# Batch 0's k and v as head pairs of nine tokens a partition, q and the first layer 1 by token halves, and the steps up to tile 1 in a written order by engine

## The chip, the cores and the metric

The kernel runs on one core of a Trainium2 chip. TensorE (PE) multiplies matrices into PSUM; VectorE (DVE), ScalarE (ACT) and GpSimd (POOL) work elementwise; SyncE (SP), ACT and POOL issue DMAs that share 16 DMA engines. Each engine takes its own instructions in the order in which they were written, and waits on semaphores of the others. The metric is the device time in microseconds (us) of the whole program.

## The reference

Inputs are q, k, v of shape (8 batches, 8 heads, 576 tokens, 64), four experts' w1 (512 x 1024) and w2 (1024 x 512), and 4608 x 4 probabilities.

```python
def phi(x):
    return np.where(x > 0, x, np.exp(x) - 1.0) + 1.0
q_p, k_p = phi(q), phi(k)
kv = np.einsum('bhsd,bhse->bhde', k_p, v)
z = np.sum(k_p, axis=2)
num = np.einsum('bhsd,bhde->bhse', q_p, kv)
den = np.einsum('bhsd,bhd->bhs', q_p, z)[..., None] + 1e-06
x = (num / den).transpose(0, 2, 1, 3).reshape(B * S, H * D)

p = domain_probs / (domain_probs.sum(-1, keepdims=True) + 1e-09)
for e in range(4):
    h = np.maximum(x @ w1[e], 0.0)
    out += p[:, e:e + 1] * (h @ w2[e])
```

So a linear attention per batch makes x (4608 tokens x 512), and four two-layer networks are run on every token and summed with the token's probabilities.

## The kernel before

The 4608 tokens are nine tiles of 512. Tile j below 8 is the first 512 tokens of batch j; the ninth collects the 64 leftover tokens of every batch. All products are in half precision.

**Attention of a batch.** q, k and v come in pieces of two heads (256 KB), four tokens a partition, and the leftovers in pieces of their own (`load`, `load_left`). phi is min(exp(x), max(x + 1, 1)): ACT makes the exp (`phi_act`), DVE the rest (`phi_dve`). `kv` multiplies k and v of a head pair into a 64 x 65 block for each head (column 65 is the sum z); ACT copies it to `kvz`. `pe_qT` transposes q on TensorE. `nd` makes numerators and denominators of a head pair and token block, `norm` divides on DVE (a reciprocal, L474, and a product, L475). `pe_xT` transposes the quotient to `xT`, which the networks read. From batch 2 on the transposes are DMAs.

**The networks.** Layer 1 of expert 0 on tile 0 is plain (`layer1_group`, L552), and so is layer 2 of all four experts on tile 0 (`layer2_part`, L607). All else is a seven-product scheme by 2 x 2 blocks: products p1 to p7 of layer 1 in `Block` (TensorE L761, copies and relus on ACT, add-relu on DVE, L745), layer 2 in `layer2_product` (L696), with sums of weights on DVE (`weight_sums` s, `weight_sums2` t), of tokens (`token_sum`, ts), and of hidden values on POOL (`hidden_sum`). `add_acc` adds a layer-2 product, scaled by the probability, to the output accumulator on DVE (L598) or, the first time, on ACT (L596).

**Weights and batch 1** are loaded by POOL, in the order of `CFG["DMA"]`: w1 of expert e in halves (`w1e0`, `w1e1`; expert 0's in quarters, `w100` to `w103`), w2 in halves (`w2e0`, `w2e1`), each converted to half precision on the way. A DMA that POOL issues takes one of eight semaphores, and waits until the DMA that had it eight issues before has landed; SP and ACT share another eight.

**What sets the order.** Nothing is scheduled by the compiler. Batch 0 is written out step by step from `CFG["B0"]` (loads) and `CFG["START"]`, where a number is that many filler matmuls on zeros (`warm`, L888) and `dma0` and `dma1` are POOL's load list. All other steps have a due position in `CFG` and are sorted by it: one list for all engines, so what a step issues on TensorE, and what ACT or DVE does with its product, stand at the same place of the list. PSUM tiles of the attention take turns in banks: `s`, `e`, `b`, `py` in the start, then `s` alone (two buffers).

Of the kernel before, what the change touches and what calls it, by code (L numbers as in the profile page):

```python
# [1 line left out]

# [8 lines left out]
FP32 = mybir.dt.float32  # L11
# [9 lines left out]
    "DMA": ('w100', 'w101', 'w102', 'w103', 'k0', 'w201', 'lk1', 'w200', 'w111', 'w110', 'w121', 'w120', 'lv0', 'lk0', 'w211', 'w210', 'v2', 'v1', 'v0', 'k1', 'w130', 'lv1', 'w131', 'q0', 'k2', 'k3', 'v3', 'w220', 'q2', 'q1', 'w221', 'q3', 'w230', 'w231'),  # L21
# [51 lines left out]
    "MODE": {'k0': 0, 'q2': 1, 'k3': 0, 'q0': 0, 'k2': 0, 'k1': 1, 'q1': 0, 'q3': 0, 'T3': 0, 'T0': 0, 'T1': 1, 'v1': 2, 'v2': 0, 'v3': 2, 'v0': 0, 'T2': 1},  # L73
    "APS": ('s', 'e', 'b', 'py'),
    "START": (11, 'qa1', 'qa0', 'ka0', 'qd1', 'lv', 'qd0', 2, 'qT1', 'kd0', 5, 'qT0', 'ka1', 'v1', 'lka', 'lkd', 'v0', 7, 'kv0', 'qa2', 'kd1', 'ka2', 'qa3', 3, 'nd0', 'kd2', 7, 'kv1', 'qd2', 'v2', 'qd3', 'dma0', 'v3', 4, 'nd1', 'qT2', 1, 'kv2', 'ka3', 3, 'xT0', 'dma1', 'kd3', 'qT3', 'nd2', 'xT1', 1, 'kv3', 'ph1', 1, 'nd3', 'ph2', 'xT2', 'xT3', 1, 'ph0'),
    "B0": ('slk', 'aq0', 'slv', 'aq1', 'sv0', 'sv1', 'sq2', 'sk2', 'ak0', 'sq3', 'sv2', 'sv3', 'ak1', 'sk3'),
    "CAST": (),
}
# [3 lines left out]
def kernel(  # L82
# [10 lines left out]
    nc = tc.nc  # L93
    CAST = CFG["CAST"]
    ATTN, HSUM, L2ORD, L2AT, MODE = (CFG[x] for x in ("ATTN", "HSUM", "L2ORD", "L2AT", "MODE"))
# [32 lines left out]
    make_identity(nc, identh)  # L128

# [14 lines left out]
    w1_sb = [pw.tile([P, DC, F], FP16, tag=f"w1_{e}", name=f"w1_{e}") for e in range(E)]  # L144
    w2_sb = [pw.tile([P, FC, Dm], FP16, tag=f"w2_{e}", name=f"w2_{e}") for e in range(E)]
# [5 lines left out]
    s1_sb = [pw.tile([P, 3, 2, F // 2], FP16, tag=f"s1_{e}", name=f"s1_{e}") for e in range(E)]  # L151


    t2_sb = {e: pw.tile([P, 3, FH, DH], FP16, tag=f"t2_{e}", name=f"t2_{e}") for e in SE}
# [9 lines left out]
    turn = {"aps": ["s", "e"], "ph": ["b", "py"]}  # L164

    def bank(kind, shape, dtype, name):
        tag = turn[kind][0]
        turn[kind] = turn[kind][1:] + [tag]
        return ppm.tile(shape, dtype, tag=tag, bufs=2, name=name)

    def aps(shape, dtype, name):
        return bank("aps", shape, dtype, name)
# [888 lines left out]
```

## Time and profile before

| | us |
|---|---|
| median of 3 runs (495.6 to 497.83) | 495.95 |
| span of the profiled execution | 494.1 |
| TensorE busy | 483.7 |
| DVE busy | 379.5 |
| POOL busy | 357.0 |
| ACT busy | 336.7 |

The page gives no time of the profiled execution beside its span; the median of the runs lies 1.85 us above it. A span is the time from the first to the last instruction on the core. A row of a timeline has start, length, engine, line, operation and tiles, and in brackets how long the engine stood idle before it and what ended that. A busy engine isn't always a useful one: fillers count, and matmuls are pipelined, so that a row's length is longer than its share of the engine. The granted clock in the profile is 1.00 in every stretch; what TensorE really did at the start is seen in the distance of its rows.

The transfers behind the start, by size and median time from issue to landing:

| issued | queue | count | KB each | us to landing |
|---|---|---|---|---|
| q, k, v pieces of later batches | SP | 26 each | 256 | 2.8 to 3.2 |
| weights in halves | POOL | 14 | 512 | 12.2 |
| w1 of expert 0 in quarters | POOL | 4 | 256 | 5.7 |

### The profile page before, as it was taken

To read this page: it belongs to the slowest core of one execution; us is meant where nothing else is said; L and a number is where in the kernel's file an instruction comes from. 1 tells how busy PE (TensorE), PEld (TensorE's weight loads), DVE (VectorE), ACT (ScalarE), POOL (GpSimd) and SP (SyncE) were. 2 spreads that over 40 slices of the span, in tenths; PEclk is the share of its full clock that TensorE was granted. 3 is DMA by queue.
4 is the path that set the end of the run, shared out by engine and by line. 5 is a ranking of instruction groups with operands and counts; after the bars stand their busy time and mean duration, and the time that the engine had idled before them with its cause. 6 is when DMAs were issued, how large, how long until landed. Compare 5 with 4: busy or idle time off the path is not lost.

```text
span 494.1 us, 11611 instructions
## 1 busy us (share of the span) xinstructions
PE 483.7 (98%) x4346; PEld 409.3 (83%) x4346; DVE 379.5 (77%) x800; ACT 336.7 (68%) x678; POOL 357.0 (72%) x344
## 2 busy tenths in 40 slices
PE   9999999999999999999999999999999999999996
PEld 3557656878898989898989898989898888888885
DVE  5639988799867987698859886888687756775686
ACT  6768969954988488848894789468954565446530
POOL 3735204878977797769776977698669877987775
PEclk9999999999999999999999999999999999999999
DMA  8999966542465234533464255523231020002003
GB/s 261 222 214 247 262 134 189 161 106 49 110 188 116 55 111 161 132 69 93 134 165 82 71 150 139 102 53 94 87 74 35 4 96 1 1 1 87 1 1 86
DMA packets 82104, 53.65 MB, mean 109 GB/s; under 512 B 46240, under 2 KB 75808, under 8 KB 82048
## 3 DMA queue, kind: packets, MB, share of 16 engines
q1 hardware_dynamic: 70512, 40.00, 31.0%
q0 software_dynamic: 9888, 11.41, 12.2%
q10 hardware_dynamic: 1648, 1.51, 1.1%
q8 instruction: 34, 0.56, 0.5%
q14 instruction: 22, 0.18, 0.1%
HBM read 45.16 MB, written 9.44 MB: 111 GB/s over the span
## 4 chain that ended last, share of the span: by engine, by line
PE 79%; DMA 11%; DVE 5%; ACT 3%; POOL 1%; issue 1%; SPq 0%; ACTq 0%; DVEq 0%
PE py L696 37%; PE pb L761 21%; PE pe L761 16%; DMA w<-in_moe_w_dram 9%; DVE acc L598 2%; PE py L607 1%; DMA rawb<-in_v_dram 1%; DVE x_sb L475 1%; PE psum_nd L492 1%; PE psum_kv L444 1%; DVE h L745 1%; POOL w L185 1%; DMA rawh<-in_q_dram 1%; PE pb L696 1%; ACT u L772 0%
## 5 line engine op out<-in xcount | busy, mean ns | idle before, releaser
L598 DVE SCALAR_TENSOR_TENSOR acc<-py,p_sb,acc 128x256 f32<-128x256 f32 (+1 forms) x382 | 182.4, 488 | 44.3 <-PE py L696 39.6
L745 DVE CUSTOM_DVE_ANT_0 h<-pe,u 128x512 f16<-128x512 f32 x140 | 96.4, 688 | 44.1 <-PE pe L761 26.1
L761 PEld LDWEIGHTS <-w 128*128 128x128 f16 x1120 | 108.9, 98 | 17.3 <-issue 1.2
L663 POOL TENSOR_TENSOR hs<-h 128x512 f16<-128x512 f16 x64 | 74.2, 1159 | 54.4 <-DVE h L745 53.3
L696 PEld LDWEIGHTS <-h 128*128 128x128 f16 x1024 | 99.6, 98 | 12.3 <-issue 0.9
L696 PE MATMUL py<-w,h 128*128 128x256 f16 x744 | 106.4, 273 | 0.0
L772 ACT COPY u<-pb 128x512 f32<-128x512 f32 x140 | 83.0, 593 | 27.4 <-PE pb L761 25.5
L665 POOL TENSOR_TENSOR hs<-hs,h 128x512 f16<-128x512 f16 x64 | 74.3, 1160 | 27.5 <-PE py L696 24.9
L761 PEld LDWEIGHTS <-s 128*128 128x128 f16 x840 | 81.6, 98 | 11.9
L761 PE MATMUL pb<-tt,w 128*128 128x256 f16 x560 | 84.0, 273 | 0.1
L696 PEld LDWEIGHTS <-hs 128*128 128x128 f16 x768 | 74.4, 98 | 8.8 <-issue 0.4
L669 POOL TENSOR_TENSOR hs<-h,hs 128x512 f16<-128x512 f16 x64 | 75.3, 1177 | 3.6 <-PE py L696 3.2
L696 PE MATMUL py<-t,hs 128*128 128x256 f16 x496 | 74.4, 273 | 0.1
L667 POOL TENSOR_TENSOR h<-h 128x512 f16<-128x512 f16 x64 | 74.3, 1162 | 0.0
L787 ACT ACTIVATE h<-pe 128x512 f16<-128x512 f32 x70 | 42.0, 600 | 45.0 <-PE pe L761 44.2
L781 ACT COPY pe<-pb 128x512 f32<-128x512 f32 x70 | 40.1, 573 | 41.6 <-PE pb L761 15.4
L805 ACT ACTIVATE h<-pb 128x512 f16<-128x512 f32 x70 | 42.1, 601 | 9.6 <-PE pb L761 9.5
L761 PE MATMUL pe<-tt,s 128*128 128x256 f16 x280 | 42.0, 273 | 0.0
L761 PE MATMUL pb<-tt,s 128*128 128x256 f16 x280 | 42.0, 273 | 0.0
L761 PE MATMUL pb<-xT,w 128*128 128x256 f16 x248 | 37.2, 273 | 0.4 <-DMA w<-in_moe_w_dram 0.4
L761 PE MATMUL pe<-xT,w 128*128 128x256 f16 x248 | 37.2, 273 | 0.3 <-ACT pe L781 0.3
L761 PE MATMUL pe<-xT,s 128*128 128x256 f16 x248 | 37.2, 273 | 0.0
(125 smaller groups left out, 609.6 us busy)
## 6 DMA issues: line engine op xcount, KB each, us to landing
out_dram<-acc SPq DMA_DIRECT2D x32, 256.0 KB, 2.5
w<-in_moe_w_dram POOLq DMA_DIRECT2D x14, 512.0 KB, 12.2
rawb<-in_v_dram SPq DMA_DIRECT2D x26, 256.0 KB, 2.8
rawb<-in_q_dram SPq DMA_DIRECT2D x26, 256.0 KB, 2.8
rawb<-in_k_dram SPq DMA_DIRECT2D x26, 256.0 KB, 3.2
w<-in_moe_w_dram POOLq DMA_DIRECT2D x4, 256.0 KB, 5.7
rawb<-in_k_dram POOLq DMA_DIRECT2D x4, 256.0 KB, 8.0
rl<-in_q_dram SPq DMA_DIRECT2D x16, 64.0 KB, 2.7
```

The costliest lines, as they stand in the source:

```text
L598: nc.vector.scalar_tensor_tensor(out=acc, in0=ps, scalar=pscal, in1=acc, op0=AO.mult, op1=AO.add)
L663: nc.gpsimd.tensor_tensor(out=hs[0], in0=a21, in1=a22, op=AO.add)
L665: nc.gpsimd.tensor_tensor(out=hs[1], in0=hs[0], in1=a11, op=AO.subtract)
L667: nc.gpsimd.tensor_tensor(out=a21, in0=a11, in1=a21, op=AO.subtract)
L669: nc.gpsimd.tensor_tensor(out=hs[3], in0=a12, in1=hs[1], op=AO.subtract)
L696: nc.tensor.matmul(out=ps, lhsT=lhsT(k), rhs=rhs[:, k], start=first and k == 0, stop=k == FH - 1, skip_group_check=True,)
L745: nc.vector._custom_dve(TENSOR_ADD_SAT, out=out, in0=ps, in1=u, s0=BIG, s1=0.0)
L761: nc.tensor.matmul(out=ps[:, kk], lhsT=lk(kc), rhs=rhs[:, kc], start=first and kk == 0 and kc == 0, stop=kc == 1, skip_group_check=True,)
L772: nc.scalar.copy(u, self.b)
L781: nc.scalar.copy(self.e5, self.b)
L787: nc.scalar.activation(self.h[:, :, 0, 0:NH], self.e5, AF.Relu)
L805: nc.scalar.activation(self.h[:, :, 1, 0:NH], self.b, AF.Relu)
```

## The change

- **Batch 0's k and v.** All 576 tokens of a head pair are one piece of 128 partitions (64 for each head) with nine tokens each, so a run of memory is 2,304 bytes and there are no leftovers of k and v to load. `kv` is nine times two matmuls of 64 x 65, one for each head, on the two halves of the partitions. The raw and converted tiles stand where the weights and weight sums of experts 2 and 3 come later. The exp is always in SBUF (`k_exp`, ACT), max(x + 1, 1) is on DVE or POOL (`k_lin`), the minimum on DVE (`k_min`), the cast of v on POOL or ACT (`v_cast`), and the copy of each head's block on ACT and DVE.
- **Batch 0's q** is loaded, mapped and transposed by token halves and four heads, in runs of 512 bytes; two of the four `q_lin` are on POOL. The transposes of x are by token halves too (`x_half`), with copies on ACT or DVE.
- **Layer 1 of expert 0 on tile 0** works by token halves (`layer1_half`): 64 matmuls of 256 columns for 32 of 512, cut where the parts of `xT` come (`CUT`).
- **Fillers**: 8, 4 and 2, for 46 before.
- **The order.** Steps are split where another engine takes over (`yield`): the TensorE part, the part on ACT or DVE, the store. `CFG["EARLY"]` names the parts one by one, from the first load to tile 1's first two experts; behind it the due positions rule as before. In it expert 1's w1 (`w110`, `w111`) is loaded right after expert 0's, ahead of both halves of expert 0's w2; before, `w201` and `w200` came first.
- **Banks.** A step's PSUM tile takes the bank named for it in `BANK`, otherwise `s`.

```diff
+    "LQ": 'SSSS',
+    "LK": 'ASSS',
+    "LV": 'SSSA',
+    "KL": 'VVPV',
+    "VC": 'PPAP',
+    "QL": 'PPVV',
+    "QT": 'AVAV',
+    "KC": ('AV', 'AV', 'AV', 'AV'),
+    "XT": ('AV', 'VV', 'AA', 'AA'),
+    "CUT": (((0, 3, 4), (0, 3, 4), (0, 4), (0, 4)), ((0, 2, 4),) * 4),
+    "WARM": (8, 4, 2),
...
+    "EARLY": (
+        "lq0 ql0 lk0 lk1 ke1 lv3 qe0 lv1 kl1 km1 warm0 lv0 qm0 warm1 lq3 vc1 w100 ke0 ql3 qT0 lq2 kv1 qT0 warm2 qe3 lk3 ke3 kv1 kl0 lq1 qe1 qm3 w102 qT3 vc0",
+        "qe2 km0 ql2 kv0 kv0 kl3 lk2 ql1 ke2 kv1 kv0 qT3 qm2 qT2 qT2 km3 lv2 w101 kl2 w103 nd10 w110 vc3 nd00 vc2 km2 nd11 w111 w200 kv2 nd00 kv2 nd10 nd11",
+        "nd01 w201 kv3 k2 kv3 xT00 w120 xT00 qm1 qT1 nd01 kv2 kv3 xT10 qT1 xT01 xT01 xT11 xT11 nd31 nd31 nd21 L21 nd30 w121 L11 nd21 L01 nd20 xT10 xT21 xT21",
+        "xT31 rv0 rv1 xT31 ts0.0 L31 L01 L11 nd30 nd20 xT20 v2 xT30 ts0.1 L31 L11 ts0.2 L01 xT20 L21 s1.0 s1.1 xT30 p1.010 s1.3 L00 L00 L31 L30 p1.011 L21 rk1",
+        "L10 L10 p1.010 p2.010 p6.010 L00 p1.011 L10 p2.011 rk0 lpr0 L20 pr0 k1 w210 p6.010 k0 k3 ts0.3 L30 v3 p2.010 p2.011 p6.011 p7.010 w211 p5.010 p7.010",
+        "s0.0 p6.011 y0.00 y0.01 p4.010 p4.010 p5.011 p7.011 c22.010 s1.2 v0 p3.010 s0.3 y0.20 y0.21 v1 L20 p3.010 p7.011 b1.k2 y0.22 p1.020 p1.020 y0.02 y0.03",
+        "y0.03 c22.011 p3.011 p4.011 p2.020 p2.020 y0.10 b1.km2 q3 y0.11 y0.12 p4.011 q0 b1.v2 w130 y0.13 y0.13 s2.0 w131 b1.lv s2.1 q2 p6.020 p1.021 p6.020",
...
-    "START": (11, 'qa1', 'qa0', 'ka0', 'qd1', 'lv', 'qd0', 2, 'qT1', 'kd0', 5, 'qT0', 'ka1', 'v1', 'lka', 'lkd', 'v0', 7, 'kv0', 'qa2', 'kd1', 'ka2', 'qa3', 3, 'nd0', 'kd2', 7, 'kv1', 'qd2', 'v2', 'qd3', 'dma0', 'v3', 4, 'nd1', 'qT2', 1, 'kv2', 'ka3', 3, 'xT0', 'dma1', 'kd3', 'qT3', 'nd2', 'xT1', 1, 'kv3', 'ph1', 1, 'nd3', 'ph2', 'xT2', 'xT3', 1, 'ph0'),
-    "B0": ('slk', 'aq0', 'slv', 'aq1', 'sv0', 'sv1', 'sq2', 'sk2', 'ak0', 'sq3', 'sv2', 'sv3', 'ak1', 'sk3'),
...
+    kraw = [pw.tile([P, 2, TK, D], FP32, tag=f"{x}_{E - 1}", name=f"kraw{x}") for x in ("s1", "t2")]
+    vraw = [pw.tile([P, 2, TK, D], FP32, tag=f"{x}_{E - 2}", name=f"vraw{x}") for x in ("s1", "t2")]
+    kpos = pw.tile([P, NPAIR, TK, D], FP16, tag=f"w1_{E - 1}", name="kpos")
+    kexp = pw.tile([P, NPAIR, TK, D], FP16, tag=f"w2_{E - 1}", name="kexp")
+    vpos = pw.tile([P, NPAIR, TK, DE], FP16, tag=f"w2_{E - 2}", name="vpos")
+    nc.gpsimd.memset(vpos[:, :, :, D:DE], 1.0 / SX)
...
-    turn = {"aps": ["s", "e"], "ph": ["b", "py"]}
-
-    def bank(kind, shape, dtype, name):
-        tag = turn[kind][0]
-        turn[kind] = turn[kind][1:] + [tag]
-        return ppm.tile(shape, dtype, tag=tag, bufs=2, name=name)
+    now = [None]
 
     def aps(shape, dtype, name):
-        return bank("aps", shape, dtype, name)
-
+        return ppm.tile(shape, dtype, tag=CFG["BANK"].get(now[0], "s"), bufs=2, name=name)
...
+    class First(Batch):
+
+        def open(self):
+            self.qp = pm.tile([P, CM, H, D], FP16, tag="h", bufs=NHB, name="qp")
+            self.qT = pa.tile([P, CM, NPAIR, P], FP16, tag="qT", bufs=1, name="qT")
+            self.x = pm.tile([P, NPAIR, CM, P], FP16, tag="tt", bufs=2, name="x_sb")
+            self.new_xT()
+
+        def load_kv(self, name, i, eng):
+            t, src = {"k": (kraw, k), "v": (vraw, v)}[name]
+            eng.dma_start(
+                out=t[i // 2][:, i % 2].rearrange("p t d -> p (t d)"),
+                in_=src[0, 2 * i : 2 * i + 2].rearrange("h (p t) d -> (h p) (t d)", t=TK),
+            )
+
+        def load_q(self, i, eng):
+            t = praw.tile([P, HG, 2, D], FP32, tag="raw", name="rawq")
+            hf, g = divmod(i, 2)
+            eng.dma_start(
+                out=t,
+                in_=q[0, g * HG : (g + 1) * HG, 0:SM].rearrange("h (p c) d -> p h c d", c=CM)[
+                    :, :, 2 * hf : 2 * hf + 2
+                ],
+            )
+            self.raw["q", i] = t
+
+        def flat(self, t, i):
+            return t[:, i].rearrange("p t d -> p (t d)")
+
+        def raw_of(self, t, i):
+            return self.flat(t[i // 2], i % 2)
+
+        def k_exp(self, i):
+            nc.scalar.activation(self.flat(kexp, i), self.raw_of(kraw, i), AF.Exp)
+
+        def k_lin(self, i, eng):
+            eng.tensor_scalar(self.flat(kpos, i), self.raw_of(kraw, i), 1.0, 1.0, AO.add, AO.max)
+
+        def k_min(self, i):
+            kp = self.flat(kpos, i)
+            nc.vector.tensor_tensor(out=kp, in0=self.flat(kexp, i), in1=kp, op=AO.min)
+
+        def v_cast(self, i, eng):
+            (eng.copy if eng is nc.scalar else eng.tensor_copy)(vpos[:, i, :, 0:D], vraw[i // 2][:, i % 2])
+
+        def q_part(self, i):
+            hf, g = divmod(i, 2)
+            return self.qp[:, 2 * hf : 2 * hf + 2, g * HG : (g + 1) * HG].rearrange("p c h d -> p h c d")
+
+        def q_exp(self, i):
+            ee = self.ph["q", i] = pm.tile([P, HG, 2, D], FP16, tag="hs0", bufs=2, name="ee")
+            nc.scalar.activation(ee, self.raw["q", i], AF.Exp)
+
+        def q_lin(self, i, eng):
+            eng.tensor_scalar(self.q_part(i), self.raw["q", i], 1.0, 1.0, AO.add, AO.max)
+
+        def q_min(self, i):
+            nc.vector.tensor_tensor(out=self.q_part(i), in0=self.ph["q", i], in1=self.q_part(i), op=AO.min)
+
+        def q_turn(self, i, eng):
+            hf, g = divmod(i, 2)
+            ps = aps([P, 2, 2, P], FP16, "psum_qT")
+            for c in range(2):
+                for a in range(2):
+                    h0 = g * HG + 2 * a
+                    nc.tensor.transpose(out=ps[:, c, a], in_=self.qp[:, 2 * hf + c, h0 : h0 + 2], identity=identh)
+            yield
+            (eng.copy if eng is nc.scalar else eng.tensor_copy)(
+                out=self.qT[:, 2 * hf : 2 * hf + 2, 2 * g : 2 * g + 2], in_=ps
+            )
+
+        def kv(self, i, engs):
+            ps = aps([P, DE], FP32, "psum_kv")
+            for t in range(TK):
+                for u in range(2):
+                    us = slice(u * HP, (u + 1) * HP)
+                    nc.tensor.matmul(
+                        out=ps[us],
+                        lhsT=kpos[us, i, t],
+                        rhs=vpos[us, i, t],
+                        start=t == 0,
+                        stop=t == TK - 1,
+                        skip_group_check=True,
+                    )
+            for u in range(2):
+                yield
+                us = slice(u * HP, (u + 1) * HP)
+                (engs[u].copy if engs[u] is nc.scalar else engs[u].tensor_copy)(
+                    out=self.kvz[us, i, u], in_=ps[us]
+                )
+
+        def x_half(self, i, hf, eng):
+            ps = aps([P, 2, P], FP16, "psum_xh")
+            for c in range(2):
+                nc.tensor.transpose(out=ps[:, c], in_=self.x[:, i, 2 * hf + c], identity=identh)
+            yield
+            (eng.copy if eng is nc.scalar else eng.tensor_copy)(
+                out=self.xT[:, i, hf * NH : (hf + 1) * NH],
+                in_=ps.rearrange("p c i -> p (c i)"),
+            )
+
+    def layer1_half(g, hf, hT, cuts):
+        ps = aps([P, 2, NH], FP32, "ph")
+        for lo, hi in zip(cuts, cuts[1:]):
+            for kk in range(2):
+                fj = 2 * g + kk
+                for dc in range(lo, hi):
+                    nc.tensor.matmul(
+                        out=ps[:, kk],
+                        lhsT=w1_sb[0][:, dc, fj * P : (fj + 1) * P],
+                        rhs=b0.xT[:, dc, hf * NH : (hf + 1) * NH],
+                        start=kk == 0 and dc == 0,
+                        stop=dc == DC - 1,
+                        skip_group_check=True,
+                    )
+            yield
+        nc.scalar.activation(hT[g % 2][:, :, g // 2, hf * NH : (hf + 1) * NH], ps, AF.Relu)
...
+        @property
+        def h(self):
+            if self.hT[self.d] is None:
+                self.hT[self.d] = new_h()
+            return self.hT[self.d]
...
         def p1(self):
-            self.h = self.hT[self.d] = new_h()
             self.b = self.bank("b")
             x = xT_of(self.j)
             self.products(self.b, lambda k: a_block(self.e, 0, 0, k), x[:, 0:2, 0:NH], True)
+            yield
             self.e5 = self.bank("e")
...
-        warm_ps = ppm.tile([P, NT], FP32, tag="py", bufs=2, name="warm_ps")
+        warm_ps = ppm.tile([P, NT], FP32, tag="e", bufs=2, name="warm_ps")
...
-        for x in CFG["START"]:
-            f, *a = (warm, x) if isinstance(x, int) else steps[x]
-            f(*a)
...
+            put_at(0, f"lq{i}", b0.load_q, i, on[CFG["LQ"][i]])
+            put_at(0, f"lk{i}", b0.load_kv, "k", i, on[CFG["LK"][i]])
+            put_at(0, f"lv{i}", b0.load_kv, "v", i, on[CFG["LV"][i]])
+            put_at(0, f"ke{i}", b0.k_exp, i)
+            put_at(0, f"kl{i}", b0.k_lin, i, on[CFG["KL"][i]])
+            put_at(0, f"km{i}", b0.k_min, i)
+            put_at(0, f"vc{i}", b0.v_cast, i, on[CFG["VC"][i]])
+            put_at(0, f"qe{i}", b0.q_exp, i)
+            put_at(0, f"ql{i}", b0.q_lin, i, on[CFG["QL"][i]])
+            put_at(0, f"qm{i}", b0.q_min, i)
+            put_at(0, f"qT{i}", b0.q_turn, i, on[CFG["QT"][i]])
+            put_at(0, f"kv{i}", b0.kv, i, [on[y] for y in CFG["KC"][i]])
+            for hf in range(2):
+                put_at(0, f"nd{i}{hf}", b0.nd, i * CM + 2 * hf, 2)
+                put_at(0, f"xT{i}{hf}", b0.x_half, i, hf, on[CFG["XT"][i][hf]])
+                put_at(0, f"L{i}{hf}", layer1_half, i, hf, hT, CFG["CUT"][hf][i])
+        for x in CFG["DMA"]:
+            put_at(0, x, load_second, x)
+        for i, n in enumerate(CFG["WARM"]):
+            put_at(0, f"warm{i}", warm, n)
...
-        for _, _, g in work:
-            g[0](*g[1:])
+        live = {name: g for _, _, name, g in work}
+        assert len(live) == len(work)
+
+        def advance(name):
+
+            now[0] = name
+            g = live[name]
+            if isinstance(g, tuple):
+                g = live[name] = g[0](*g[1:]) or iter(())
+            if next(g, live) is live:
+                del live[name]
+
+        for name in " ".join(CFG["EARLY"]).split():
+            advance(name)
+        for name in [w[2] for w in work]:
+            while name in live:
+                advance(name)
 
 
 # ---- launch: one core; inputs and outputs as the reference has them ----
```

## The prediction

> **What bounds the kernel now.** I read the page first (shares of busy time), then the busy time of every engine in stretches, then the timelines of TensorE, VectorE (DVE), ScalarE (ACT) and GpSimd (POOL) up to 120 us, the chain that ended last, and the transfers.
>
> The page, then busy time by stretch; columns are the stretch, its length, and busy us with counts for PE, weight load, DVE, ACT and POOL, then clock, DMA share and GB/s:
>
> ```profile
> PE 483.7 (98%) x4346; PEld 409.3 (83%) x4346; DVE 379.5 (77%) x800; ACT 336.7 (68%) x678; POOL 357.0 (72%) x344
> ```
>
> ```profile
> 0.00:20.00 20.00, 18.55 (x119) 9.37 (x120) 13.40 (x39) 12.93 (x28) 11.47 (x26) 1.00 1.07 248
> 20.00:30.00 10.00, 10.00 (x47) 4.38 (x45) 1.36 (x6) 6.12 (x11) 3.68 (x6) 1.00 1.18 213
> 30.00:60.00 30.00, 29.25 (x224) 20.86 (x224) 26.61 (x44) 26.33 (x54) 12.23 (x17) 1.00 1.18 247
> 60.00:65.00 5.00, 4.54 (x34) 2.79 (x35) 3.50 (x6) 4.38 (x10) 0.00 (x0) 1.00 1.21 213
> 65.00:70.00 5.00, 3.83 (x32) 1.94 (x30) 4.61 (x16) 1.70 (x3) 0.00 (x0) 1.00 0.86 192
> 70.00:100.00 30.00, 29.64 (x247) 22.22 (x246) 25.15 (x43) 28.82 (x64) 17.87 (x16) 1.00 0.49 146
> 100.00:115.00 15.00, 13.89 (x136) 12.22 (x134) 14.33 (x33) 8.28 (x18) 10.62 (x10) 1.00 0.53 111
> 115.00:400.00 285.00, 284.88 (x2707) 256.21 (x2705) 228.17 (x493) 204.51 (x416) 230.35 (x209) 1.00 0.39 99
> ```
>
> TensorE is the bound from 115 us on, and nothing of the change lies there. Before that its busy share hides much, because fillers (`warm`) count as busy. So I count useful time: four 256-column matmuls take 0.44 us in the chain, 0.1094 us per 256 columns; all matmuls but the fillers, by shape and start time, make 467.0 us. The span is 494.1, so 27.1 us are lost: 15.2 up to 20 us, 1.9 from 20 to 65, 2.1 from 65 to 70, 2.5 from 70 to 115, 0.8 from there to the last matmul at 489.5, and 4.6 behind it. The change can only touch the first four, 21.7 us.
>
> TensorE's first rows, the end of batch 0's dependent work, and two stalls behind it:
>
> ```profile
> 1.19 5.58 PE L888 MATMUL warm_ps<-qz 128*128 128x512 f16 x13 [1.19 <-DVE qz L134]
> 6.83 1.24 PE L888 MATMUL warm_ps<-qz 128*128 128x512 f16 x5
> ...
> 19.96 6.21 PE L552 MATMUL ph<-xT,w 128*128 128x512 f16 x28
> 30.50 0.61 PE L761 MATMUL pb<-xT,w 128*128 128x256 f16 x4 [0.44 <-DMA w<-in_moe_w_dram]
> ```
>
> ```profile
> 30.54 0.69 DVE L633 TENSOR_TENSOR s<-w 128x1024 f16<-128x1024 f16 x1 [8.51 <-DMA w<-in_moe_w_dram]
> ```
>
> ```profile
> 60.83 1.45 PE L607 MATMUL py<-w,h 128*128 128x512 f16 x6 [0.47 <-DMA w<-in_moe_w_dram]
> ...
> 68.00 0.29 PE L492 MATMUL psum_nd<-kvz,qT 128*128 128x130 f16 x2 [0.26 <-DVE x_sb L475]
> ```
>
> The reader sees: layer 1 runs dense only from 19.96; DVE stands idle 8.51 us because expert 1's first-layer weights come after expert 0's second layer; a weight is late at 60.8; and batch 1's numerators each wait for DVE's division of the one before. From 30 to 115 us DVE is busy 74.2 us of 85 (the five rows above), so it is nearly a second bound.
>
> **The change part by part.**
>
> *Batch 0's loads.* Before: twelve 256 KB pieces in 1 KB runs and four 64 KB leftover pieces in 256-byte runs. The last k piece, issued at 8.37, lands 5.6 us later, at 13.95. From 4 to 8 us, with leftovers in flight, 283 GB/s moved; from 8 to 12, without, 348. After: eight k and v pieces of 288 KB in 2,304-byte runs, no leftovers for k and v, and four q pieces in 512-byte runs. 2.36 MB at 348 takes 6.8 us and 1.05 MB at 283 to 348 takes 3.0 to 3.7; from the first packets at about 2 us that ends at 12 to 12.5. But POOL now issues w100 and w102 behind its q step and its cast of v pair 1, at about 6.5 us instead of 10.16, so 0.5 MB written goes between: 2.7 us, by the 1.35 us a piece that four of them show (5.7 us to landing each, issued 0.8 us apart). The last v thus lands at 12 to 14.8; I take 14. SP issues the last q, k and v pieces only as lq0, lk1 and lv1 land, and ACT issues lv3 behind the exp of k pair 1; SP's issues before were paced in the same way (5.0 to 8.9 us), and the DMA engines are full meanwhile (share 1.07), so these waits cost nothing unless the queue runs dry, 0.7 us for a piece. Batch 2's loads on SP keep their number and wait for the same buffers.
>
> *What follows the last load.* POOL carries three `tensor_scalar` steps and three v casts now, with seven weight issues of 0.75 us between them. A cast of 512 costs it 0.67; a two-operand step 1.16. For a `tensor_scalar` that the trace does not show I take 0.7 (it has one input, like the cast); 1.16 is the other end, 1.4 us more over three. The cast of v pair 3 stands behind w103 and w110: about 16 us. Then 18 matmuls of kv (0.5 to 1 us), two copies (0.27 and about 0.2), numerators and division (0.13 + 0.55 for each half pair), transpose and copy (0.4): layer 1 is dense at 18 to 20, I take 19. ACT waits in its order too: for the exp of k pair 3 (its DMA at about 9.5) with q's and kv's copies queued behind. By token halves, 16 matmuls of layer 1 (1.75 us) can go before pairs 2 and 3 are there. Useful by then: 6.2 us against 4.8. Lost: 19 less 6.2 is 12.8, but 0.9 of the 6.2 is new work (kv has 72 matmuls of 65 columns for 20 of 130: 2,080 columns more). Net against 15.2: -1.5, range -2.5 to +0.5 at full clock. I take -0.7, as two engines wait in order for DMAs there.
>
> *Fillers.* 46 become 14, 32 x 0.22 = 7 us of TensorE. They stood in idle time, so their price is nothing while that idle time lasts. What they cover is the clock: the first 13 ran at 0.43 us each, the next five at 0.22, so the clock doubled at about 6.4 us. The 12 fillers at the head end at 6.3; then come sparse groups until about 16 us. [...] From its rows alone: half rate lasted 5.1 us of continuous work, so the other end is +2.6; the near end is 0. I take 0, since groups of kv and transposes stand every 2 to 3 us.
>
> *Weights in a new order.* w110 and w111 come right after expert 0's first layer; then w200, w201. A piece takes 2.46 us (0.52 MB at 213 GB/s). With w103 landing at 18 to 19.5, w111 is there at 23 to 24.5, not at 30.5. TensorE needs w110 after 8.1 us of useful work and w111 after 11.6, so with 14.5 lost at 22.6 and 26.1: no wait. The 0.44 goes. w221 stands earlier in POOL's list and is needed later (after 48.9 useful us instead of 43.6), so the 0.47 goes as well: -0.9, range -0.9 to 0.
>
> *DVE.* Its sums start 6 to 7 us sooner; its own work grows by 1.5 to 2.3 (four kvz copies, three xT copies of 0.28, pieces of 576 instead of 512). If DVE is what holds the stretch to 115, it ends 4 us sooner. In exchange more sums stand ahead of each add-relu (L836): 4 to 7 us of DVE work more before the same product in tile 1's first units. So I do not book all 4.
>
> *Batch 1's numerators.* They now take turns in four banks and stand between products. Of the 2.1 lost between 65 and 70 I book -1.5 (0 to -2). Of the 2.5 between 70 and 115 (ACT at 28.8 of 30, then DVE at 14.3 of 15) I book -1.0 (+2 to -2): ACT has 2.3 us less to do in all, DVE's gain is above.
>
> *Kv's extra columns*, +0.9. Layer 1 as 64 x 256 columns instead of 32 x 512 is the same columns. The tail is untouched.
>
> **Sum**: -0.7 - 0.9 - 1.5 - 1.0 + 0.9 = -3.2. The profiled execution had a span of 494.1; the median of the three runs, 495.95, lies 1.85 above it for what is around a span. 490.9 + 1.85 = 492.75.
>
> **The rivals.**
> *A: DVE and ACT become no sooner free.* The planned order is tight: if in-order waits give DVE as much idle time by 60 us as before (18.6 us, from the rows above), TensorE's loss at batch 1's numerators is that plus the 2.7 us by which DVE's work is ahead of TensorE's there, 21.3, and with the 0.9 the result is about what it was: -1 to +1, 496. For it: both engines over 85% busy from 30 to 115. Against: DVE's largest idle row was a DMA that now comes sooner.
> *B, slower: the clock falls at the start.* It halves between 8 and 16 us. Then batch 0's kv, numerators and transposes run at half rate (about 5 useful us, half of it in the chain: +2.5), layer 1 pays 2.6, and DVE and ACT get their inputs that much later: -3.2 + 5.1 + about 1 = +3, 499. It decides once TensorE rests for longer than any rest of before, with less than +3.2 it is only a smaller gain.
> *C: the order works fully.* The loss stays at about 14.8 us through 115: with 0.8, 4.6 and 0.9 of new columns that is 21.1 for the 27.1 of now: -6.0, 490. For it: no weight is then late. Against: ACT's and DVE's rows are full.
>
> **How the numbers follow.** Forecast 492.75 (491 to 495): 0.45; C 0.20; A 0.18; B 0.17. A measurement here tells 0.5%, 2.5 us, from no change: faster is below 493.5. All of C, two thirds of the forecast's: 0.50. Same: the other third, most of A: 0.28. Slower: B and a little of A: 0.22. The range leaves out the outer ends of B and C: 488 to 499.5.
>
> **What would show it.** Right: the sums of expert 1 (L730) start by 24.5 us; layer 1 (L640) is dense by 19 to 20 with 0.11 us per 256 columns; no weight is waited for at 60 us; DVE's idle time by 60 us is under 16; from 65 to 70 TensorE loses under 1 us; tile 1's products come 3 us sooner. Wrong: matmuls of layer 1 at 0.21 us; idle TensorE behind kv copies of ACT at 30 to 50 us; DVE rows that wait in order while TensorE waits for a later one.

## The result and the profile after

The changed kernel takes 498.25 us (median; 497.99 to 498.71), the kernel before 495.97 in the same comparison: a ratio of 1.0040, 95% interval 1.0022 to 1.0058. It is slower by 2.3 us, where 3.2 us less were forecast. The profiled execution has a span of 496.7 us (494.1 before).

The page of the changed kernel, busy engines and the granted clock in 40 slices:

```profile
PE 479.4 (97%) x4398; PEld 412.3 (83%) x4398; DVE 380.2 (77%) x804; ACT 333.0 (67%) x671; POOL 362.8 (73%) x345
...
PEclk9599999999999999999999999999999999999999
```

TensorE is busy 4.3 us less, because 32 fillers (7 us) are gone, and the clock shows a 5 in the second slice (12.4 to 24.8 us), where the kernel before had 9 throughout. Busy time by stretch, with columns as before (the clock is the third number from the end):

```profile
0.00:20.00 20.00, 11.85 (x115) 6.52 (x116) 11.14 (x31) 8.74 (x17) 15.32 (x23) 0.76 0.95 228
20.00:30.00 10.00, 9.99 (x82) 8.36 (x81) 7.88 (x24) 4.63 (x11) 5.26 (x8) 0.79 1.16 201
30.00:60.00 30.00, 29.78 (x223) 20.39 (x221) 20.13 (x34) 26.83 (x55) 13.74 (x19) 1.00 1.15 243
60.00:65.00 5.00, 5.00 (x49) 3.97 (x48) 4.86 (x13) 4.92 (x11) 0.00 (x0) 1.00 1.20 221
65.00:70.00 5.00, 5.00 (x54) 3.89 (x52) 4.62 (x13) 3.92 (x7) 0.00 (x0) 1.00 1.19 229
70.00:100.00 30.00, 26.84 (x206) 18.61 (x203) 26.47 (x44) 26.15 (x58) 14.17 (x13) 1.00 0.60 158
100.00:115.00 15.00, 14.88 (x145) 13.46 (x146) 13.00 (x29) 7.93 (x18) 11.49 (x11) 1.00 0.29 76
115.00:400.00 285.00, 284.12 (x2700) 255.31 (x2698) 227.56 (x491) 205.13 (x416) 229.42 (x208) 1.00 0.39 99
```

From 60 to 70 us TensorE is now full (5.00 of 5.00 twice, for 4.54 and 3.83), and from 70 to 100 it has 3.2 us of rest, where it had 0.4.

Counted as in the prediction (useful time: every matmul but the fillers, 0.1094 us per 256 columns; the rest of the elapsed time is lost), the profiled executions of the two kernels and of a faster one found below ("all four edits") come to this, in us:

| | before | changed | all four edits |
|---|---|---|---|
| useful | 467.0 | 467.9 | 467.9 |
| lost up to 30 us | 15.3 | 18.7 | 16.0 |
| lost 30 to 80 us | 4.6 | 0.3 | 0.8 |
| lost 80 to 130 us | 2.0 | 5.0 | 2.6 |
| lost from 130 us to the last matmul | 0.6 | 0.4 | 0.6 |
| behind the last matmul | 4.6 | 4.4 | 4.4 |
| span | 494.1 | 496.7 | 492.3 |

So the change does win 4.3 us in the middle, but pays 3.4 at the start and 3.0 behind 80 us, and 0.9 of new columns. TensorE's rows at the start (length, then idle time before the row and what ended it):

```profile
9.54 0.40 PE L598 MATMUL psum_qT<-identh,qp 128*128 128x128 f16 x4 [0.84 <-DVE qp L590]
10.43 0.69 PE L609 MATMUL psum_kv<-vpos,kpos 64*64 64x65 f16 x18 [0.49 <-POOL vpos L576]
...
16.79 0.70 PE L609 MATMUL psum_kv<-vpos,kpos 64*64 64x65 f16 x18 [1.63 <-DVE kpos L573]
...
18.43 0.71 PE L609 MATMUL psum_kv<-vpos,kpos 64*64 64x65 f16 x18 [0.61 <-POOL vpos L576]
...
20.75 1.06 PE L640 MATMUL ph<-xT,w 128*128 128x256 f16 x4
21.61 0.43 PE L475 MATMUL psum_nd<-kvz,qT 128*128 128x130 f16 x2
21.82 1.92 PE L640 MATMUL ph<-xT,w 128*128 128x256 f16 x8
...
24.16 1.66 PE L640 MATMUL ph<-xT,w 128*128 128x256 f16 x12
```

The kv of pair 2 starts at 16.79 and that of pair 3 at 18.43, both behind GpSimd's work. Layer 1 starts at 20.75 and takes 1.92 us for eight matmuls, where twelve take 1.66 from 24.16 on: half rate. The clock was 1.00 from 7.1 to 10.5 us, 0.50 from there to 24.1, and 1.00 from then on. GpSimd's rows, and the row of VectorE that links the step at 13.85 to the kv of pair 2:

```profile
4.71 1.92 POOL L587 TENSOR_SCALAR qp<-rawq 128x512 f16<-128x512 f32 x1 [3.28 <-DMA rawq<-in_q_dram]
...
11.14 1.92 POOL L587 TENSOR_SCALAR qp<-rawq 128x512 f16<-128x512 f32 x1 [0.76 <-DMA rawq<-in_q_dram]
...
13.85 2.39 POOL L569 TENSOR_SCALAR kpos<-krawt 128x576 f16<-128x576 f32 x1
...
17.69 0.69 POOL L576 CAST vpos<-vrawt 128x576 f16<-128x576 f32 x1
```

```profile
16.27 0.46 DVE L573 TENSOR_TENSOR kpos<-kexp,kpos 128x576 f16<-128x576 f16 x1 [2.02 <-POOL kpos L569]
```

The three `tensor_scalar` steps take 6.23 us together. VectorE's first sum of expert 1's weights, and TensorE's longest waits from 30 to 135 us:

```profile
26.39 0.69 DVE L730 TENSOR_TENSOR s<-w 128x1024 f16<-128x1024 f16 x1 [0.74 <-DMA w<-in_moe_w_dram]
```

```profile
PE psum_nd L475 <- DMA qT<-qp: 2.2, 1, 2.2
PE psum_nl L493 <- DMA qz<-qlp: 0.9, 1, 0.9
PE psum_kv L439 <- ACT vp L353: 0.7, 1, 0.7
```

No weight is waited for any more. What is waited for is batch 2: its transposed q (at 100.1 us), its leftover q (122.5), its v (85.4).

### The profile page after: what moved, and what is told of

It reads as the page before. It is cut to its first block, busy times and chain, and to the rows that moved or that the text cites. A ratio compares the mean times of both kernels' runs of the same rounds, so it can differ in the third digit from the quotient of the medians.

```text
span 496.7 us, 11695 instructions
## 1 busy us (share of the span) xinstructions
PE 479.4 (97%) x4398; PEld 412.3 (83%) x4398; DVE 380.2 (77%) x804; ACT 333.0 (67%) x671; POOL 362.8 (73%) x345
## 3 DMA queue, kind: packets, MB, share of 16 engines
q0 software_dynamic: 9888, 11.41, 12.4%
## 4 chain that ended last, share of the span: by engine, by line
PE 90%; DMA 4%; ACT 2%; POOL 1%; DVE 1%; issue 0%; SPq 0%; ACTq 0%
PE py L795 38%; PE pb L852 23%; PE pe L852 18%; PE py L700 4%; DMA rawq<-in_q_dram 2%; PE ph L640 2%; PE psum_nd L475 1%; PE psum_kv L439 1%; DMA qT<-qp 1%; DVE acc L691 1%; DMA rawb<-in_k_dram 1%; PE pb L795 1%; POOL kpos L569 0%; DMA qz<-qlp 0%; POOL qp L587 0%
## 5 line engine op out<-in xcount | busy, mean ns | idle before, releaser
L764 POOL TENSOR_TENSOR hs<-hs,h 128x512 f16<-128x512 f16 x64 | 73.9, 1155 | 25.0 <-PE py L795 22.6
L768 POOL TENSOR_TENSOR hs<-h,hs 128x512 f16<-128x512 f16 x64 | 74.2, 1160 | 3.6 <-PE py L795 3.2
L795 PE MATMUL py<-w,hs 128*128 128x256 f16 x248 | 37.2, 273 | 0.0
```

The costliest lines, as they stand in the source:

```text
L764: nc.gpsimd.tensor_tensor(out=hs[1], in0=hs[0], in1=a11, op=AO.subtract)
L768: nc.gpsimd.tensor_tensor(out=hs[3], in0=a12, in1=hs[1], op=AO.subtract)
L795: nc.tensor.matmul(out=ps, lhsT=lhsT(k), rhs=rhs[:, k], start=first and k == 0, stop=k == FH - 1, skip_group_check=True,)
```

## The experiments

Times are medians with the range of the runs; ratios are to the kernel before, run beside it on the same chip, with 95% intervals. "Lost at 30 us" and the like are from the profiled execution.

### The start: clock, GpSimd, loads

**Fillers.** Five more groups, 23 fillers, put into the rests of the start:

```diff
-    "WARM": (8, 4, 2),
+    "WARM": (8, 4, 2, 3, 2, 9, 6, 3),
-  w102 qT3 ... ql2 kv0 kv0 ... qm2 qT2 ... w200 kv2 ... w201 kv3
+  w102 warm3 qT3 ... ql2 warm4 kv0 kv0 ... qm2 warm5 qT2 ... w200 warm6 kv2 ... w201 warm7 kv3
```

> The changed kernel with 23 more fillers (3, 2, 9, 6 and 3) put into rests of TensorE between 8.6 and 18.5 us. Clock theory (the halved clock from 10.5 to 24.1 us costs time by itself): the clock stays whole, the 12 half-length matmuls of layer 1 and the kv groups behind 18.4 us run at 0.11 and 0.027 us instead of 0.21 and 0.04, TensorE has lost about 17 us at 25 us instead of 18.7, and the time falls by 1.0 to 2.0 us, to 496.3 to 497.3. Rival (POOL's slow steps set the start, TensorE only waits for DVE's divisions behind them): the clock is whole and the time falls by less than 0.5 us, 497.8 to 498.5. If fillers stand in the way: above 498.5.

Measured: 501.53 us (501.39 to 502.01), ratio 1.0115 (1.010 to 1.013). The clock stayed at 1.00 up to 30 us, and 17.3 us were lost by then for 18.7, 1.4 us fewer, as expected. The same start without added fillers lost 17.6 to 18.7 us by 30 us in the six profiled executions that have it (`after`, `e3`, `e6`, `e9`, `e11`, `f2`), the less the sooner its half rate ended (at 21.6 to 24.1 us), and with them 17.1 to 17.3 in two; so the clock's price there is 0.3 to 1.6 us, by execution. But by 85 us the gain was gone (20.15 lost, exactly the changed kernel's figure), and then the wait for batch 2's q was 2.81 us instead of 2.17, with half rate for 3.4 us behind it. The time fell where the third branch puts it (above 498.5, "the fillers stand in the way"), though at 30 us they did not stand in the way.

**No `tensor_scalar` on GpSimd.**

```diff
-    "KL": 'VVPV',
+    "KL": 'VVVV',
-    "QL": 'PPVV',
+    "QL": 'VVVV',
```

> The changed kernel with its three tensor_scalar steps of POOL (two of q, one of k, 1.92, 1.92 and 2.39 us) on DVE instead (0.4 to 0.5 us each). POOL theory: all four quarters of expert 0's first weights are issued by 13 us instead of 16.2, kv of pair 2 starts at 13.5 to 14.5 instead of 16.8 and of pair 3 at 14 to 15 instead of 18.4; layer 1 is dense 2 to 3 us sooner and the time falls by 2 to 3 us, to 495.3 to 496.3. Clock theory alone (POOL only fills idle time): the clock still halves, and the time falls by less than 0.7 us. Third view, transfers set the start: the weights of expert 1 land within 0.5 us of now and TensorE has as much lost at 40 us.

Measured: 496.42 us (494.04 to 498.7), ratio 1.0005 (0.999 to 1.002): 1.8 us faster than the change, a little less than the 2 to 3 us expected. VectorE's rows for the three steps that GpSimd had done:

```profile
4.52 0.43 DVE L587 TENSOR_SCALAR qp<-rawq 128x512 f16<-128x512 f32 x1 [2.02 <-DMA rawq<-in_q_dram]
...
11.40 0.85 DVE L587 TENSOR_SCALAR qp<-rawq 128x512 f16<-128x512 f32 x1
...
14.03 0.45 DVE L569 TENSOR_SCALAR kpos<-krawt 128x576 f16<-128x576 f32 x1
```

```profile
18.95 1.06 PE L640 MATMUL ph<-xT,w 128*128 128x256 f16 x4
```

0.43 and 0.85 us for 1.92 each, and 0.45 for 2.39; layer 1 starts 1.8 us sooner (18.95 for 20.75), and 16.6 us are lost at 30 us for 18.7. The clock was halved in this start too, up to 21.6 us.

**Batch 2's leftover loads (`b1.next`, which stands among batch 1's steps) behind batch 2's piece** on SyncE's queue, which stood still at them from 57 to 72 us:

```diff
-  p4.020 b1.next b1.km1 ...
+  p4.020 b1.km1 ... b1.load4 b1.next s3.1
```

> The changed kernel with one step moved in the written order: SP's six leftover loads of batch 2 (b1.next), which stop SP's queue from 57 to 72.4 us until their buffer is free, come behind five loads that now wait behind them. Queue theory: k, v and the probabilities are issued by 58 us instead of 76 to 79, ACT's wait for k (1.36 us) goes, batch 2's kv waits for nothing at 85 us (0.66) and its transposed q comes 1 to 2 us sooner than 100.07, so that TensorE's wait of 2.17 us shrinks below 1: the time falls by 1.2 to 2.5 us, to 495.7 to 497.0. Rival (DVE and ACT hold this stretch anyway): the loads come early, the wait at 98 to 100 us stays within 0.5 us of 2.17 and the time falls by less than 0.7 us.

Measured: 498.5 us (495.39 to 500.31), ratio 1.0044 (1.0025 to 1.0062): no change. The wait for v at 85 us was gone (19.3 lost at 90 us for 20.4), but TensorE then reached batch 2's numerators that much sooner and waited for q as long as before; its clock was halved behind that wait.

**All three together.**

> The three edits together: fillers, tensor_scalar steps on DVE, SP's leftover loads later. If the three causes add up: TensorE has lost 14 to 15 us at 25 us instead of 18.7, and the time is 491.5 to 493.5, below the kernel before by 2.5 to 4.5 us. If they hide one another (transfers of expert 1's weights or DVE are late next): 494 to 496. If none of them is the cause: 498.

Measured: 497.01 us (495.06 to 499.1), ratio 1.0019 (1.0004 to 1.0033). The edits are not additive. In the profiled execution, one of the slower ones (498.48), 16.9 us were lost at 90 us, 3.5 fewer than in the change, but 22.9 at 130, only 1.1 fewer. TensorE's rows in between:

```profile
97.28 0.44 PE L475 MATMUL psum_nd<-kvz,qT 128*128 128x130 f16 x4 [2.95 <-DMA qT<-qp]
97.52 1.05 PE L852 MATMUL pb<-xT,w 128*128 128x256 f16 x4
...
100.07 1.02 PE L795 MATMUL py<-w,hs 128*128 128x256 f16 x4
100.93 0.60 PE L852 MATMUL pb<-tt,s 128*128 128x256 f16 x4
```

A wait of 2.95 us, and then 0.85 us from group to group instead of 0.44 until 100.9: the clock record is at 0.50 there, which costs another 1.7 us. In this execution most of what was won at the start is lost at this one place.

**The kernel before without 33 of its 46 fillers.**

> The kernel before with its first 13 filler matmuls kept and the 33 others left out. Theory of the clock: with the long rests of its start no longer filled, the granted clock is halved between 8 and 20 us, and the kernel loses 1.4 us or more at the start: 497.3 to 499. Rival: the old start's own work comes densely enough that the clock stays at 1.0, the fillers are worth nothing: 495.6 to 496.2.

Measured: 495.8 us (495.5 to 496.8), ratio 0.9995 (0.9986 to 1.0003). The time is the rival's, but not for its reason; busy time by stretch:

```profile
10.00:20.00 10.00, 8.17 (x61) 5.80 (x60) 7.46 (x24) 6.87 (x17) 9.40 (x14) 0.54 1.30 254
20.00:30.00 10.00, 9.71 (x48) 4.42 (x48) 2.15 (x9) 6.42 (x11) 3.81 (x6) 1.00 1.17 211
```

The clock is halved from 10 to 20 us and the time is the same. The half clock was over when layer 1 got dense, at 20.67 us for 19.96 in the kernel before; in the changed kernel it lasted 3.4 us into layer 1. It was not quite free: 16.0 us were lost at 30 us for 15.3. But at 65 us it was 16.9 for 17.0: the waits for weights that the kernel before has in between were shorter by as much.

### The stretch from 95 to 125 us

In the written order batch 2's numerators (`b2.nd4`) stand right behind the step that starts the transposition they read (`b2.qT`), which takes 4.3 to 5.2 us to land in the changed kernel.

**Numerators eight products later**, in the change, with all three edits, and without GpSimd's steps alone:

```diff
-  b2.qT b2.nd4 b2.nd5 p3.110 p4.110 m10.60 p1.120 b2.nd5 b2.nd4 p5.111 m10.51 ...
+  b2.qT p3.110 p4.110 m10.60 p1.120 p5.111 m10.51 ... m10.70 p3.111 b2.nd4 b2.nd5 m10.61 m10.31 b2.nd5 b2.nd4 p3.111 m10.31 ...
```

> The changed kernel with one edit: in the written order batch 2's numerators (nd4, nd5, then nd1, nd2, nd0) stand up to eight products later; in the change nd4 stands right behind the step qT that starts the transposition it reads. Theory: what the start gains or loses is levelled at 100 us because TensorE meets these numerators before the transposition of q, 4.7 us long, has landed (2.17 us of idle time in the changed kernel's profile, 2.1 to 3.0 in all four kernels run so far). Eight products of 0.44 us are 3.5 us of work, more than the wait: it goes, the loss at 130 us falls from 24.0 to 21.7, and the time from 498.25 to 496.0 (495.5 to 496.7). Rival: the numerators' results are needed as early as before, so that the wait comes back at tile 2's first products: no change, 497.8 to 498.6.

> The kernel with all three edits (fillers at the start, no tensor_scalar steps on GpSimd, the leftover loads behind batch 2's) and the numerators' later place as well. Theory: there the wait was 2.95 us, and matmuls behind it ran at 0.21 us for 256 columns for 3.4 us (clock 0.50 in the records), 1.7 us more; with the eight products ahead both go, the loss at 130 us falls from 22.9 to about 18.3, and the time from 497.0 to 492.5 (492 to 493.5), 0.7% below the kernel before. Rival: a further wait behind it takes half or more of that: 494.5 or above.

> The kernel without tensor_scalar steps on GpSimd (no fillers added, the leftover loads in their place) and the numerators' later place. Theory: 2.2 us of wait goes, and the scatter over its runs, 494.0 to 498.7, shrinks, as it came from whether the clock was halved behind that wait: 494.2 (493.5 to 495). Rival: the scatter and the time stay, 496.0 to 496.9, as the start makes them.

Measured: 498.38 us (497.09 to 498.96), ratio 1.0041 (1.0025 to 1.0057); 495.55 (494.57 to 497.82), 0.9989 (0.9976 to 1.0003); and 496.23 (494.4 to 497.29), 0.9998 (0.9985 to 1.0012). Three times the rival. The wait for q was gone from all three, and another had come; the kernel with all three edits waited for:

```profile
PE py L795 <- DVE acc L691: 1.6, 3, 1.1
PE psum_nl L493 <- DMA qz<-qlp: 1.4, 2, 1.0
```

The divisions (the second `b2.nd5 b2.nd4`) now stood on VectorE ahead of the output sum of `m10.31`, and TensorE waited for that. With all three edits 15.73 us were lost at 30 us, and 15.84 with GpSimd's steps gone and no fillers added, where the half rate ended at 19.2 us, just before layer 1. Without GpSimd's steps, then, the halving costs little when it ends before layer 1; in `e2`, where it ran to 21.6, the loss was 16.6, up to 0.9 more than with fillers.

**The place mended in full**: divisions behind the sums, and batch 3's leftover loads behind the transposition of batch 2's leftover q, which had waited on SyncE's queue behind them. The first pair of lines is against the kernel with the numerators later, the second against the change:

```diff
-  ... m10.70 p3.111 b2.nd4 b2.nd5 m10.61 m10.31 b2.nd5 b2.nd4 p3.111 m10.31 p1.121 b2.nd1 p4.111 ...
+  ... m10.70 p3.111 b2.nd4 b2.nd5 m10.61 m10.31 p3.111 m10.31 p1.121 b2.nd5 b2.nd4 p4.111 ... m10.71 b2.nd1 ...
-  b2.next p2.130 m11.31 c22.121 b2.qTl
+  p2.130 m11.31 c22.121 b2.qTl b2.next
```

> The changed kernel with the written order of the 95 to 125 us stretch mended in three places: batch 2's numerators eight products later, their divisions on VectorE behind the output sums that TensorE waits for (in the run with the numerators later alone, those divisions stood ahead of them and TensorE waited 1.4 us for the sums instead), and the leftover loads of batch 3 behind the transposition of batch 2's leftover q (TensorE waited 0.9 us for it at 122 us). Theory: all that the changed kernel loses between 90 and 130 us (3.5 us) is the place of these steps in the list: the loss at 130 us falls from 24.0 to 21.0, the time from 498.25 to 495.3 (494.8 to 496.0). Rival: engines other than TensorE are full there, and the waits only pass on: 497.0 or more.

Measured, in the changed kernel: 497.39 us (495.98 to 499.04), ratio 1.0028 (1.0016 to 1.0039): 0.9 us faster than the change where 3 were expected; by its time it is the rival's (497.0 or more). Its profiled execution, one of the shorter ones (496.53 us), lost 22.1 at 130 us for 24.0; 0.7 of these 1.9 it was already ahead at 30 us, where the edit changes nothing and its half rate ended sooner (22.6).

> The same mended order together with the three earlier edits (fillers at the start, no tensor_scalar steps on GpSimd, batch 1's leftover loads behind batch 2's pieces). With the numerators later alone these made 495.6, and lost 16.9 us by 95 and 21.3 by 130. Theory of the places: the loss at 130 falls to 18.5, the time to 492.8 (492.2 to 493.6), 0.6% below the kernel before. Rival: 494.8 or more.

Measured, with the three edits as well: 494.03 us (493.38 to 494.5), ratio 0.9957 (0.9945 to 0.997). This beats both kernels, by 2.0 and 4.2 us, though not by all that was expected. What TensorE still waits for from 30 to 140 us:

```profile
PE psum_nd L475 <- DVE x_sb L463: 1.1, 1, 1.1
PE pe L852 <- ACT h L885: 0.4, 1, 0.4
PE py L795 <- DVE acc L691: 0.3, 1, 0.3
PE pb L852 <- ACT u L863: 0.2, 1, 0.2
```

The three edits made 1.2 us by themselves, the mended place 0.9, both together 4.2. The mended place with GpSimd's steps gone but no fillers added, and with fillers but GpSimd's steps kept, were not measured; so how much of the 4.2 us is the fillers' stays open.

**The written order ended at 72 us**, with the due positions of the list for all that follows:

> The changed kernel with its written order ended ahead of batch 2's first k step (TensorE's time 72 us); all later steps go by their due positions, as in the kernel before. Theory: it is the written order behind 72 us that loses, 5.0 us from 80 to 130 where the due positions of the kernel before lose 2.1; so the loss at 130 falls from 24.0 to about 21, and the time from 498.25 to 495.3 (494.5 to 496.3). Rival: the loss there comes from TensorE's being ahead of ScalarE and VectorE, whatever the order: 497.5 or more.

Measured: 501.92 us (500.38 to 504.81), ratio 1.0124 (1.0101 to 1.0148). The expectation that the old positions would do better there was wrong; the rival was right in its time. TensorE waited 4.6 us in two pieces (up to 73.7 and 80.5 us) for output sums, and lost 3.5 from 80 to 130 us for 5.0 in the change:

```profile
PE py L688 <- DVE acc L679: 4.6, 2, 2.5
```

That the old positions fit the old start and not this one is a likely reason that no run shows.

### Copies for transpositions

Four kernels with every DMA transposition replaced by a plain DMA copy of as many bytes, so that the wait for q shrinks without any step being moved. These kernels leave the transposing out, and what reads q then gets untransposed values: they serve to measure time alone. One of the four kinds of transposition as an example:

```diff
-            nc.sync.dma_start_transpose(
-                out=self.qT.rearrange("p c a i -> p (c a) i"),
+            nc.sync.dma_start(
+                out=self.qT.rearrange("p c a i -> p (c a i)"),
                 in_=self.qp.rearrange("p c h d -> p (c h d)"),
```

> The kernel before with every transposition by DMA (q, leftover q, quotients and leftover quotients of the batches from the third on) replaced by a plain DMA copy of as many bytes; the transposing itself is left out, so that the networks read untransposed values. It gives the three kernels beside it their zero. The kernel before waits 0.5 us for such a transposition: 495.0 to 495.9.

> The changed kernel with the same DMA copies for transpositions (the transposing left out). Theory: of its later loss, 2.2 us are a wait for the transposition of q, 4.7 us long, and 0.9 us one for the leftover q's; a copy lands sooner (2 to 3 us), so 1.5 to 3 us of it go: 495.3 to 496.8, within 1 us of the kernel before with copies. Rival: the waits come from ScalarE's and VectorE's steps ahead of them, and stay: 497.5 or more.

> The changed kernel with copies for transpositions and the 23 added fillers at the start. With the transpositions the fillers took 1.4 us from the loss at 30 us and the time rose by 3.3. Theory: the halved clock of 10 to 24 us costs 1.4 us, which a later wait took back; with copies in its place it reaches the end: 1 to 1.8 us under the changed kernel with copies. Rival: the gain at the start is lost later by whatever comes next: no difference, or slower.

> The changed kernel with copies for transpositions and GpSimd's three tensor_scalar steps on VectorE. With the transpositions that made 1.8 us (498.25 to 496.4). Theory: GpSimd's steps cost 2 us at the start, by 30 us, and all of it reaches the end where no transposition is waited for: 1.8 to 2.4 us under the changed kernel with copies, and not over the kernel before with copies. Rival: half of it or more is lost later, 1 us or less.

| with copies | us | ratio to before | lost at 30 us | lost 80 to 130 us |
|---|---|---|---|---|
| kernel before | 496.19 | 1.0005 (0.9996 to 1.0014) | 15.3 | 2.0 |
| changed kernel | 495.51 | 0.9988 (0.9977 to 0.9999) | 17.7 | 2.7 |
| and fillers | 498.86 | 1.0063 (1.0044 to 1.0082) | 17.1 | 6.2 |
| and no `tensor_scalar` on GpSimd | 492.87 | 0.9939 (0.9921 to 0.9956) | 15.5 | 2.1 |

The kernel before was 0.3 us slower than expected of it. A copy of q lands in 3.3 us (median) instead of 4.7. The copies take 2.7 us from the changed kernel and nothing from the kernel before. In the profiled executions the loss from 80 to 130 us falls by 2.3 of the 3.0 us that the change had lost there, and TensorE's wait for batch 2's q from 2.17 to 0.85: the late q (and the leftover q) are most of the loss behind 80 us. The 1.0 us less at 30 us goes with a half rate that ended sooner in this execution (at 22.4 us); DMAs transpose from batch 2 on only, so the copies don't bear on it. GpSimd's steps cost 2.2 us at the start, and 2.6 at the end: where no long wait stands behind, none of it is lost on the way. Without them and without the wait the change is 3.3 us ahead of the kernel before with the same copies. The fillers again lost more than they won. In that profiled execution the copy of q took 5.6 us to land, and:

```profile
100.29 0.61 PE L475 MATMUL psum_nd<-kvz,qT 128*128 128x130 f16 x4 [3.00 <-DMA qT<-qp]
100.70 1.06 PE L852 MATMUL pb<-xT,w 128*128 128x256 f16 x4
```

A wait of 3.0 us and half rate behind it once more.

Why the copy took 2 us longer there, the traces show in part. Besides the program's own DMAs they have small loads of instructions for the engines, 34 of 16 KB in the changed kernel (queue q8). With added fillers batch 2's q took 5.4 us to land in `e1` and the copy 5.6 in `f3`; without, it took 4.7 in the changed kernel and the copy 3.4 in `f2`. In the changed kernel such a load starts at 101.9 us, 1.8 us after q has landed. In `e1` the DMAs moved 7 GB/s from 98 to 99 us, within the transfer; in the changed kernel they moved 208 in the same microsecond. So what the fillers lose at this place likely has a cause that neither theory named, a longer transfer. That the added matmuls moved a load of instructions onto it, and that the load lengthened it, is the author's estimate from these numbers; no run moves the load alone.

## Why the prediction was wrong

**The start, "-0.7 (range -2.5 to +0.5)": wrong by 5 us, the largest error.** Net of new columns it was +4.3 (18.7 + 0.9 - 15.3). Three steps failed.
- "For a `tensor_scalar` that the trace does not show I take 0.7 [...]; 1.16 is the other end." It measured 1.92, 1.92 and 2.39: 6.2 us for 2.1 assumed, outside both bounds. The nearest row was taken to be the cast, because both have one input; the step has two operations and also changes the type. By the runs this is worth 1.8 us (with transpositions) to 2.6 us (with copies).
- "Useful by then: 6.2 us." The prediction let 16 matmuls of layer 1 (1.75 us) go ahead of pairs 2 and 3. In the written order the first of them stands behind the kv of pair 3, and in every kernel with this order none came sooner, so only 4.0 us of useful work are done when layer 1 starts. Even in the kernel with all four edits, where it starts at 19.5 us as forecast, 4.4 us were done by 20 us. So the start without GpSimd's steps and at full clock still lost 16.0 us, not 12.8.
- The 0.9 us of new columns were counted as a cost inside this term and once more in the sum. That made the forecast 0.9 us too slow, not too fast.

**Fillers, "I take 0, since groups of kv and transposes stand every 2 to 3 us": the reason was wrong, and the price was small at 30 us.** The clock was halved at 10.5 us all the same, though no rest among the groups since 7.1 us had been longer than 0.84. By 30 us it cost 0.3 to 1.6 us where GpSimd made layer 1 late, and at most 0.9 without GpSimd's steps, the less the sooner half rate ended. The 5.1 us behind the forecast's other end, and behind the 2.6 us of rival B, are the first fillers of the kernel before, at 0.43 us each. What the halving costs at the end stays open. Added fillers made the kernel slower twice, but there the transfer of q was longer too (5.4 us for 4.7, a copy 5.6 for 3.4). Between executions of the same kernel (41 executions of `e3`, `e6`, `e9` and `f2`, which have the changed start and no added fillers; half rate worked out from each one's mean clock) each microsecond of half rate went with 0.30 us of time (0.15 to 0.45); this is a correlation, which doesn't show that one causes the other.

**70 to 115 us, "-1.0 (+2 to -2)": wrong in sign, +3.0 from 80 to 130.** It was priced by how busy ScalarE and VectorE are. What decided was a chain that the prediction never followed: batch 2's q, from SyncE's loads through ScalarE and VectorE to a transposition of 4.7 us, whose readers stand right behind it in the written order. The order gave the wait no cover. It was 2.1 to 2.2 us in the change, in `e2` and in `e3`, and 2.8 to 3.0 in `e1` and `e4`, whose transfers took longer. With it gone and the place behind it mended, the gains at the start came through (1.2 us without, 4.2 with).

**Weights, "-0.9", and batch 1's numerators, "-1.5": right, and together undersized.** No weight is waited for at 60 us, and TensorE loses nothing from 65 to 70 us. From 30 to 80 us 4.3 us were won. w111 was late against the forecast (expert 1's sums start at 26.39, not by 24.5) without harm to TensorE.

**DVE**: its idle time by 60 us is 20.9 us (60 less 11.1, 7.9 and 20.1), not under 16. Tile 1's products come no sooner, as the start's loss eats the middle's gain.

**The rivals.** B (the clock halves, +3, 499) came nearest in time, and its event took place. But its price didn't: at 30 us the clock was at most 1.6 of the loss, for 5.1 and "about 1" there. It named neither GpSimd's steps nor the later stretch. What the forecast described, 3.2 us less, is what the change does with two things taken out that it had not seen, GpSimd's steps and the wait for transposed q: 492.87 for 496.19 with copies.

## What to carry to other kernels

Price an operation that the trace doesn't show by what it computes as well as by its inputs, and let the range reach to several times the nearest row where none is alike; three such steps on an engine that also issues the weights cost about 2 us here. Where an order is written out, look for every reader that stands right behind the step that starts its slow transfer: such a place can take back what is won ahead of it, so gains have to be tried together with it, not one at a time. And a wait that is moved must be followed on every engine that its steps touch: here moving the matmuls alone only handed the wait to VectorE's sums. Before a slower time is put down to an edit's purpose, look at what else it moved: with the added matmuls the transfer of q took 5.4 us for 4.7.

## What the runs showed of the hardware

**GpSimd's two-operation `tensor_scalar`** (fp32 to fp16, 128 x 512) takes 1.92 us in the changed kernel, where its cast of 128 x 576 takes 0.69 to 0.95; VectorE does the same step in 0.43 to 0.89 in `e2`. So GpSimd took 2.2 to 4.5 times VectorE's time for this step.

**Half rate came behind short rests.** In `e3`, batch 2's wait left TensorE without work for 2.26 us (from the end of its last group at 96.71 to 98.97) and half rate followed for 3.4 us; a rest of 2.33 us in the changed kernel (97.78 to 100.11) was followed by full rate. So the length of the rest alone doesn't decide at this size; rests of 2.97 us (`e1`) and 3.11 us (`e4`) were both followed by half rate. The halving at 10.5 us in the changed kernel came among groups of matmuls with rests of 0.84 us at most since 7.1 us. What does decide was not shown.

**A transfer was often longer when a load of instructions fell into it.** In the traces of the two kernels, transpositions of q took 4.3 to 4.7 us without a load of 16 KB (seven of them) and 4.3 to 5.6 with one (five, four of them above 5.0). That the load is the cause is argued from this.
